# Two state-space heads in one kernel: k loaded in blocks of 32 partitions, a shift convolution by channel halves, and another instruction order

## The chip, the cores and the metric

The kernel runs on one core of a Trainium2 chip. Its time is the device time in microseconds of one execution; three executions of the kernel before gave a median of 419.54 us (419.09 to 419.80). The core's engines are TensorE (PE; PEld is its weight load), VectorE (DVE), ScalarE (ACT), GpSimd (POOL) and SyncE (SP), which here only issues DMAs.

## The reference

Two independent heads over 2048 time steps, 640 channels each; their outputs are concatenated.

```python
def A(x, ...):                       # S5 head: 640 complex states
    Lam_bar = exp(dt * Lam); B_bar = ((Lam_bar - 1) / Lam)[:, None] * Bmat
    Bu = einsum("bld,pd->blp", x, B_bar)
    h[t] = Lam_bar * h[t-1] + Bu[t]                 # scan over 2048 steps
    return 2 * einsum("blp,dp->bld", h, Cmat).real + x * Dskip
def B(q, k, v, shift_k, ssm_k, ssm_D):   # H3 head
    k_shift[t] = sum over 4 taps of k[t - j] * shift_k[:, j]
    kv = k_shift * v
    y = irfft(rfft(kv, 4096) * rfft(ssm_k, 4096))[:2048] + kv * ssm_D
    return q * y
```

## The kernel before, in words

**Everything lies in one SBUF tile, `arena`,** cut by hand into named columns (`LAY`). A recording layer (`Program.add`) takes each operation with the engines that may do it, and a table (`ORDER`) of entries such as `33G0` gives the order in which all operations are emitted: operation 33, on engine G (POOL), in PSUM bank 0. Each engine and the one DMA queue (SP's) run their entries strictly in this order. The profile names all of SBUF `arena` and all of PSUM `acc`; operations are told apart by their lines.

**Head A.** x is loaded as 16 blocks (`load_x`), transposed on PE, and B is scaled and transposed (`prep_B`, L497). The scan is a tree over 16 steps: on the way up, `up2`, `up1`, `up0` project x (L508, 200 matmuls of 512 columns) and combine neighbours (L527); `coarse` (L587 to L611) scans the 128 block totals by DVE; on the way down `down` (L628, L630, evicted at L646 and L648) spreads them; then `project` makes 16 output blocks C0 to C15 (L662, L667, evicted at L671, stored at L674). Its matrix C is first reordered in DRAM (L463) and transposed by a DMA (L464).

**Head B** is a long convolution by a two-step Fourier transform, done in two halves of 320 channels (0 and 1). Per half: the filter h is loaded (`load_h`, L716) and gets the skip weight D added (L705 loads it); `s1` (L793, evicted at L798) and `s2` (L811, evicted at L824) transform it; k and v are loaded (`load_k`, L729 and L732; `load_v`, L741); `conv` does the four taps and the product with v in 16 DVE operations (L767, L772, L773; one of the 32 stands on POOL); `s1`, `s2` transform kv; `product` (L835 to L842) multiplies spectra; `r2` (L856, evicted at L861) and `r1` (L877, with q at L889) go back, and four stores (L901) write a block. Called s1h, s1k, s2h, s2k with the half behind: s1k0 is the first step of kv in half 0.

**A tile of k or v has 4 blocks of 32 partitions,** one per 80 channels; a partition holds 64 time steps (and for k the 3 steps ahead of them, its overlap). Partition 0 of a block has no steps ahead of it: `load_k` zeroes them, loads partitions 1 to 31 of each block with their overlap in one DMA of 31x67 runs of 160 bytes (L729), and the 64 steps of the four first partitions in one DMA with a partition step of 32 (L732). `load_v` (L741) is a DMA of 32x64 such runs per block. Both halves use the same tiles, as do their taps (`T`). kv overwrites v, so that the weights of s1k are read with a step of 80 elements (160 bytes).

**Waits.** Eight DMA semaphores (DMAHW0 to DMAHW7) are given to the DMAs in turn, so each DMA waits until the one eight places ahead of it has landed.

Of the kernel before, what the change touches and what calls it, by code (L numbers as in the profile page):

```python
# [137 lines left out]
def act(n):  # L138
    return 0.20 + 0.00083 * n


def dve(n, rate=1.04):
    return 0.18 + 0.00104 * n * rate / 1.04
# [47 lines left out]
def setup(c):  # L191
# [62 lines left out]
    for ch in range(4):  # L254
# [12 lines left out]
        P.add("w_s", {A: 1.07}, lambda e, qc=qc, wo=wo: e.activation(out=wo, in_=qc, func=FN.Sin, bias=npi, scale=SC13),  # L267
# [20 lines left out]
    for ch in range(4):  # L288
# [6 lines left out]
        P.add("g_q", {G: 3.4}, lambda e, qc=qc: e.tensor_tensor(out=qc, in0=qc, in1=bc(f41s, [128, 1024]), op=ALU.mult),  # L295
              outs=[full], ins=[full, f41s])
        P.add("g_s", {A: 1.07}, lambda e, qc=qc: e.activation(out=sn, in_=qc, func=FN.Sin, scale=SC), outs=[sn], ins=[full])
        for el in range(2):
            go = Gt[:, ri, 32 * bh:32 * bh + 32, el, :]
            P.add("g_k", {V: .55, G: 1.3}, lambda e, go=go, el=el: e.tensor_scalar(  # L300
# [4 lines left out]
def params(c):  # L305
# [122 lines left out]
class PartA:  # L428
# [223 lines left out]
    def project(self, i):  # L652
# [21 lines left out]
        P.add(f"st_A{i}", {PSP: .17}, lambda e: e.dma_start(out=dst, in_=ys), ins=[ys], nbytes=128 * 1280)  # L674


class PartB:
    def __init__(self, c):
# [30 lines left out]
    def load_h(self, hf):  # L709
        c, P = self.c, self.c.P  # L710
        H = self.h[hf].rearrange("p (g b) -> p g b", b=64)
        for e_ in range(4):
# [3 lines left out]
            P.add(f"ld_h{hf}", {PSP: 2.9}, lambda e, d=d, src=src: e.dma_start(out=d, in_=src), outs=[d], nbytes=80 * 4096)  # L716
# [3 lines left out]
    def load_k(self, hf):  # L720
# [4 lines left out]
        for e_ in range(4):  # L725
            c0 = 320 * hf + 80 * e_
            d = K[32 * e_ + 1:32 * e_ + 32]
            src = bass.AP(self.k2.tensor, 61 * 640 + c0, [[64 * 640, 31], [640, 67], [1, 80]])
            P.add(f"ld_k{hf}", {PSP: 2.4}, lambda e, d=d, src=src: e.dma_start(out=d, in_=src), outs=[d], nbytes=31 * 67 * 160)  # L729
        d = K[0:128:32, 3:67, :]  # L730
        src = bass.AP(self.k2.tensor, 320 * hf, [[80, 4], [640, 64], [1, 80]])
        P.add(f"ld_k{hf}", {PSP: .35}, lambda e: e.dma_start(out=d, in_=src), outs=[d], nbytes=256 * 160)  # L732

    def load_v(self, hf):
        c, P = self.c, self.c.P
        Vt = self.vt[hf].rearrange("p (b g) -> p b g", g=80)
        for e_ in range(4):
# [3 lines left out]
            P.add(f"ld_v{hf}", {PSP: 2.4}, lambda e, d=d, src=src: e.dma_start(out=d, in_=src), outs=[d], nbytes=32 * 64 * 160)  # L741
# [11 lines left out]
    def conv(self, hf):  # L753
        c, P = self.c, self.c.P
        K = self.kt[hf].rearrange("p (b g) -> p b g", g=80)
        Vt = self.vt[hf].rearrange("p (b g) -> p b g", g=80)
        T1 = self.T[:, 2560:5120].rearrange("p (b g) -> p b g", g=80)
        T2 = self.T[:, 5120:7680].rearrange("p (b g) -> p b g", g=80)
        cost = {PDVE: dve(2560, .52), PPOOL: 5.6}
        for hb in range(2):  # L760
            b0 = 32 * hb
            t1, vv = T1, Vt[:, b0:b0 + 32]

            def tap(out, j):
# [8 lines left out]
            P.add(f"cv{hf}v", cost, lambda e, t1=t1, vv=vv: e.tensor_tensor(out=vv, in0=t1, in1=vv, op=ALU.mult), outs=[vv], ins=[t1, vv])  # L773

    def s1(self, what, hf, u):
# [19 lines left out]
        P.add(f"s1{what}{hf}_{u}", {PPE: .25}, mm, ins=lh + [c.F1], group=g, nmm=32)  # L795
# [5 lines left out]
    def s2(self, what, hf, ks):  # L801
# [12 lines left out]
        P.add(f"s2{what}{hf}_{ks[0]}", {PPE: 4 * n * .0345 + .02}, mm, ins=ins, group=g, nmm=4 * n)  # L814
# [29 lines left out]
    def r2(self, hf, u):  # L844
# [14 lines left out]
        P.add(f"r2{hf}_{u}", {PPE: .47}, mm, ins=ins, group=g, nmm=16)  # L859
# [4 lines left out]
    def r1(self, hf, bs):  # L864
# [20 lines left out]
        P.add(f"r1{hf}_{bs[0]}", {PPE: 8 * n * .0086 + .03}, mm, ins=ins, group=g, nmm=8 * n)  # L885
# [226 lines left out]
```

## Time and profile before

| | |
|---|---|
| median of 3 runs | 419.54 us (419.09 to 419.80) |
| the profiled execution's own time | 421.19 us |
| its span, first to last instruction | 419.4 us |
| PE busy / PEld | 233.0 / 162.7 us (56% / 39%) |
| DVE, ACT, POOL busy | 176.0, 148.1, 47.6 us (42%, 35%, 11%) |
| mean granted TensorE clock | 0.75 of full speed |
| DMA | 24.06 MB, 57 GB/s over the span |

The profiled execution took 1.8 us more than its span and 1.65 us more than the median, so a span is near the median of runs. An engine's idle time is put down to what released it; "SPq" is the queue's own issuing of DMAs, which counts as waiting, not as busy time. In two long stretches no engine computes.

### The profile page before, as it was taken

To read this page: it belongs to the slowest core of one execution; us is meant where nothing else is said; L and a number is where in the kernel's file an instruction comes from. 1 tells how busy PE (TensorE), PEld (TensorE's weight loads), DVE (VectorE), ACT (ScalarE), POOL (GpSimd) and SP (SyncE) were. 2 spreads that over 40 slices of the span, in tenths; PEclk is the share of its full clock that TensorE was granted. 3 is DMA by queue.
4 is the path that set the end of the run, shared out by engine and by line. 5 is a ranking of instruction groups with operands and counts; after the bars stand their busy time and mean duration, and the time that the engine had idled before them with its cause. 6 is when DMAs were issued, how large, how long until landed. Compare 5 with 4: busy or idle time off the path is not lost.

```text
span 419.4 us, 7914 instructions
## 1 busy us (share of the span) xinstructions
PE 233.0 (56%) x3576; PEld 162.7 (39%) x3576; DVE 176.0 (42%) x213; ACT 148.1 (35%) x175; POOL 47.6 (11%) x47
## 2 busy tenths in 40 slices
PE   3389899800000052998000000796696689999685
PEld 3355455500000021587000000554565578777563
DVE  5956810000000899254000000589794642299532
ACT  3659467400000310443000000685477543364421
POOL 5701300000000430000000000804104000000000
PEclk9969999965555565696555555799598886899989
DMA  6970000000005900061070002209270321032315
GB/s 200 228 107 7 18 17 17 17 15 15 21 15 84 131 0 9 15 85 21 15 163 15 15 15 41 41 0 169 37 125 15 59 64 50 2 107 68 95 34 143
DMA packets 96661, 24.06 MB, mean 57 GB/s; under 512 B 90996, under 2 KB 96628, under 8 KB 96628
## 3 DMA queue, kind: packets, MB, share of 16 engines
q1 hardware_dynamic: 96598, 23.56, 30.2%
q8 instruction: 28, 0.46, 0.5%
q14 instruction: 5, 0.04, 0.0%
q10 hardware_dynamic: 30, 0.00, 0.0%
HBM read 16.68 MB, written 6.88 MB: 56 GB/s over the span
## 4 chain that ended last, share of the span: by engine, by line
SPq 36%; PE 35%; DVE 12%; ACT 8%; issue 5%; DMA 2%; POOL 0%; ACTq 0%; POOLq 0%; DVEq 0%
SPq L729 16%; PE acc L662 11%; PE acc L793 7%; SPq L741 5%; SPq L700 5%; SPq L716 5%; SPq L464 4%; PE acc L811 4%; PE acc L508 3%; PE acc L856 3%; DVE arena L767 3%; DVE arena L772 2%; DMA arena<-in_B_k_dram 2%; ACT arena L824 2%; PE acc L628 2%
## 5 line engine op out<-in xcount | busy, mean ns | idle before, releaser
L824 ACT CAST arena<-acc 128x960 bf16<-128x960 f32 (+1 forms) x39 | 35.1, 916 | 89.0 <-DMA arena<-in_B_k_dram 68.5
L767 DVE TENSOR_TENSOR arena<-arena 128x2560 bf16<-128x2560 bf16 x16 | 26.0, 1643 | 79.9 <-POOL arena L706 79.6
L508 PE MATMUL acc<-arena 128*128 128x512 bf16 x200 | 53.9, 425 | 1.6 <-DVE arena L483 1.6
L628 PE MATMUL acc<-arena 128*128 128x512 bf16 (+2 forms) x47 | 16.3, 368 | 67.8 <-ACT arena L824 67.8
L662 PE MATMUL acc<-arena 128*128 128x320 bf16 x320 | 52.5, 316 | 0.0
L798 ACT CAST arena<-acc 128x1024 bf16<-128x1024 f32 x32 | 31.7, 1019 | 37.9 <-PE acc L793 37.9
L527 PE MATMUL acc<-arena 128*128 128x128 bf16 (+2 forms) x100 | 11.9, 254 | 53.2 <-DMA arena<-in_B_k_dram 53.2
L824 DVE CAST arena<-acc 128x960 bf16<-128x960 f32 (+1 forms) x7 | 7.1, 1012 | 71.8 <-DMA arena<-in_B_k_dram 66.5
L793 PE MATMUL acc<-arena 64*64 64x64 bf16 x1280 | 35.6, 264 | 2.4 <-DVE arena L243 1.7
L662 PEld LDWEIGHTS <-arena 128*128 128x128 bf16 x320 | 30.7, 103 | 13.4 <-issue 0.2
L793 PEld LDWEIGHTS <-arena 64*64 64x64 bf16 x1280 | 33.1, 189 | 6.9 <-issue 3.9
L811 PE MATMUL acc<-arena 128*64 128x160 bf16 x512 | 26.8, 262 | 13.8 <-DVE arena L600 13.0
L630 PEld LDWEIGHTS <-arena 128*128 128x128 bf16 x50 | 5.4, 110 | 71.4 <-issue 68.9
L295 POOL TENSOR_TENSOR arena<-arena 128x1024 int32<-128x1024 int32 x4 | 7.6, 1892 | 204.1 <-DMA arena<-in_B_k_dram 204.1
L508 PEld LDWEIGHTS <-arena 128*128 128x128 bf16 x200 | 20.1, 106 | 26.9 <-issue 10.4
L527 PEld LDWEIGHTS <-arena 128*128 128x128 bf16 x100 | 7.5, 100 | 57.9 <-issue 55.2
L811 PEld LDWEIGHTS <-arena 128*64 128x64 bf16 x512 | 22.2, 126 | 19.5 <-issue 18.4
L571 ACT CAST arena<-acc 128x256 bf16<-128x256 f32 (+1 forms) x9 | 3.7, 424 | 57.6 <-DMA arena<-in_B_k_dram 55.9
L856 PE MATMUL acc<-arena 64*128 64x128 bf16 x320 | 15.8, 264 | 11.3 <-ACT arena L861 4.8
L671 ACT CAST arena<-acc 128x640 bf16<-128x640 f32 x14 | 9.7, 692 | 32.1 <-PE acc L667 32.1
L861 ACT CAST arena<-acc 128x1024 bf16<-128x1024 f32 x14 | 14.1, 1015 | 16.4 <-PE acc L856 16.4
L889 DVE TENSOR_TENSOR arena<-acc,arena 128x960 bf16<-128x960 f32 (+1 forms) x12 | 12.2, 1043 | 16.8 <-PE acc L877 16.8
(134 smaller groups left out, 336.0 us busy)
## 6 DMA issues: line engine op xcount, KB each, us to landing
out_dram<-arena SPq DMA_DIRECT2D x32, 160.0 KB
arena<-in_B_k_dram SPq DMA_DIRECT2D x8, 324.5 KB
arena<-in_A_x_dram SPq DMA_DIRECT2D x16, 160.0 KB
arena<-in_B_ssm_k_dram SPq DMA_DIRECT2D x8, 320.0 KB
arena<-in_B_v_dram SPq DMA_DIRECT2D x8, 320.0 KB
arena<-in_B_q_dram SPq DMA_DIRECT2D x8, 320.0 KB
arena<-in_A_B_re_dram SPq DMA_DIRECT2D x2, 400.0 KB
arena<-in_A_B_im_dram SPq DMA_DIRECT2D x2, 400.0 KB
```

The source lines that it names most:

```text
L508: e.matmul(o, lhsT=self.BT[:, j, d, :], rhs=self.XT[:, d, t0:t0 + n], start=(d == 0), stop=(d == 4), skip_group_check=True)
L628: e.matmul(B[:, o:o + 128 * k], lhsT=c.I3[:, 0:128], rhs=A[:, j, m + q:m + q + k, 0:128], start=True, stop=False, skip_group_check=True)
L662: e.matmul(B[:, 512 * b:512 * b + 320], lhsT=lh[j], rhs=self.CT[:, j, 320 * b:320 * b + 320], start=(j == 0), stop=False, skip_group_check ...
L700: P.add("ld_sk", {PSP: .2}, lambda e, d=d, src=src: e.dma_start(out=d, in_=src), outs=[d], nbytes=128 * 640)
L716: P.add(f"ld_h{hf}", {PSP: 2.9}, lambda e, d=d, src=src: e.dma_start(out=d, in_=src), outs=[d], nbytes=80 * 4096)
L729: P.add(f"ld_k{hf}", {PSP: 2.4}, lambda e, d=d, src=src: e.dma_start(out=d, in_=src), outs=[d], nbytes=31 * 67 * 160)
L767: P.add(f"cv{hf}m", cost, lambda e: e.tensor_tensor(out=out, in0=k, in1=bc(s, [128, 32, 80]), op=ALU.mult), outs=[out], ins=[k, c.SK[:, hf ...
L793: e.matmul(B[64 * b:64 * b + 64, 512 * l + 64 * i:512 * l + 64 * i + 64], lhsT=lh[i][ps], rhs=F[ps, b, :], start=True, stop=True, tile_pos ...
L798: P.add(f"e1{what}{hf}_{u}", {PACT: act(1024), PDVE: dve(1024)}, lambda e, B: c.CP[e](out=out, in_=B.rearrange("p (l n k s) -> p k s l n", ...
L811: e.matmul(B[64 * s:64 * s + 64, 512 * b + 160 * i:512 * b + 160 * i + 160], lhsT=c.W[:, k, 64 * b:64 * b + 64], rhs=self.AS[:, k, 160 * s ...
L824: c.CP[e](out=out, in_=b.rearrange("p r (k j n) -> p r k j n", k=n, j=4) if nj > 1 else b.rearrange("p r (k x) -> p r k x", k=n))
L856: e.matmul(B[:, 512 * s + 128 * i:512 * s + 128 * i + 128], lhsT=lh[i][s][r], rhs=rh, start=(r == 0), stop=(r == 1), tile_position=(64 * s ...
```

## The change

Three edits. In `load_k`, four DMAs of 32 partitions and 64 steps take the place of the four of 31 partitions and of the one for the first partitions; four small DMAs (`ld_kh`, L734) load the overlap of partitions 1 to 31. In `conv`, an operation takes all 64 steps of 40 channels where it took 32 steps of 80; kv goes to `T` (two areas) and not over v, and s1k reads its weights there with a step of 40 elements (80 bytes). Third, the planning costs are other numbers (in many lines, which do nothing at run time) and so is the `ORDER` table.

```diff
 def act(n):
-    return 0.20 + 0.00083 * n
+    return 0.16 + 0.000833 * n
...
+        self.kv = [v("T", 2560, 2560), v("T", 0, 2560)]
...
         for e_ in range(4):
             c0 = 320 * hf + 80 * e_
-            d = K[32 * e_ + 1:32 * e_ + 32]
-            src = bass.AP(self.k2.tensor, 61 * 640 + c0, [[64 * 640, 31], [640, 67], [1, 80]])
-            P.add(f"ld_k{hf}", {PSP: 2.4}, ...)
-        d = K[0:128:32, 3:67, :]
-        src = bass.AP(self.k2.tensor, 320 * hf, [[80, 4], [640, 64], [1, 80]])
-        P.add(f"ld_k{hf}", {PSP: .35}, ...)
+            d = K[32 * e_:32 * e_ + 32, 3:67, :]
+            src = self.k2.rearrange("(a b) d -> a b d", b=64)[:, :, c0:c0 + 80]
+            P.add(f"ld_k{hf}", {PSP: 1.6}, ...)
+        for e_ in range(4):
+            d = K[32 * e_ + 1:32 * e_ + 32, 0:3, :]
+            src = bass.AP(self.k2.tensor, 61 * 640 + 320 * hf + 80 * e_, [[64 * 640, 31], [640, 3], [1, 80]])
+            P.add(f"ld_kh{hf}", {PSP: .5}, ...)
...
-        for hb in range(2):
-            b0 = 32 * hb
-            t1, vv = T1, Vt[:, b0:b0 + 32]
+        for h in range(2):
+            t1 = self.kv[h].rearrange("p (b n) -> p b n", n=40)
+            hs = slice(40 * h, 40 * h + 40)
+            vv = Vt[:, :, hs]
...
-                k = K[:, 3 - j + b0:3 - j + b0 + 32, :]
+                k = K[:, 3 - j:67 - j, hs]
...
-            P.add(f"cv{hf}v", cost, ... tensor_tensor(out=vv, in0=t1, in1=vv, op=ALU.mult), outs=[vv], ins=[t1, vv])
+            P.add(f"cv{hf}v", cost, ... tensor_tensor(out=t1, in0=t1, in1=vv, op=ALU.mult), outs=[t1], ins=[t1, vv])
...
-            K = self.vt[hf].rearrange("p (b g) -> p b g", g=80)
-            lh = [K[:, :, x] for x in gs]
+            lh = [self.kv[x // 40].rearrange("p (b n) -> p b n", n=40)[:, :, x % 40] for x in gs]
...
 ORDER = (
-    "33G0 76V0 100G0 0G0 160S0 79S0 25V0 115V0 101G0 80S0 6G0 9V0 10V0 7V0 26V0 54V0 55V0 8V0 12V0 77A0 1G0 2V0 78S0 81T0 24V0 3V0 "
+    "48G0 0G0 111V0 115V0 151S0 25V0 76V0 99G0 14V0 154S0 112V0 1G0 27V0 100G0 6G0 113V0 114V0 77A0 38G0 24V0 80A0 43G0 7V0 54V0 8V0 "
...
```

What the table moves is seen in three places. Line numbers from L705 on are one to three higher in the kernel after.

**SP, the first half's k and v.** In the queue's order before, behind the filter loads (the semaphores that an issue waits for stand in brackets):

```order
L729 DMA arena<-in_B_k_dram 31x67x80 [waits DMAHW6_49,Activation_49]
L729 DMA arena<-in_B_k_dram 31x67x80 [waits DMAHW7_49]
L729 DMA arena<-in_B_k_dram 31x67x80 [waits DMAHW0_49]
L700 DMA arena<-in_B_shift_k_dram 128x1x320 [waits DMAHW1_49]
L729 DMA arena<-in_B_k_dram 31x67x80 [waits DMAHW2_49]
L741 DMA arena<-in_B_v_dram 32x64x80 [waits DMAHW3_49]
L732 DMA arena<-in_B_k_dram 4x64x80 [waits DVE_49,DMAHW4_49,Activation_49,Pool_49]
L741 DMA arena<-in_B_v_dram 32x64x80 [waits DMAHW5_49]
```

and after, again behind the filter loads (two more k loads, one `ld_kh` and two v loads follow, and one of the two DMAs of C stands among them):

```order
L730 DMA arena<-in_B_k_dram 32x64x80 [waits DMAHW5_49,Activation_49]
L743 DMA arena<-in_B_v_dram 32x64x80 [waits DMAHW6_49]
L453 DMA arena<-in_A_x_dram 128x640 [waits DMAHW7_49]
L743 DMA arena<-in_B_v_dram 32x64x80 [waits DMAHW0_49]
L734 DMA arena<-in_B_k_dram 31x3x80 [waits DMAHW1_49,Pool_49]
L734 DMA arena<-in_B_k_dram 31x3x80 [waits DMAHW2_49]
L730 DMA arena<-in_B_k_dram 32x64x80 [waits DMAHW3_49]
L730 DMA arena<-in_B_k_dram 32x64x80 [waits DMAHW4_49]
L734 DMA arena<-in_B_k_dram 31x3x80 [waits DMAHW5_49]
L701 DMA arena<-in_B_shift_k_dram 128x1x320 [waits DMAHW6_49]
```

The DMA with a partition step of 32 (4x64x80), which waited for three engines, is gone from k; the load of D (4x80, not shown) has the same step and remains.

**ACT, an eviction of the up pass** (L571, `ev_up0c_4`, which writes no part of k). Before, it waits for semaphore DMAHW4, whose holder is the 4x64x80 load above:

```order
L571 CAST arena<-acc 128x2x128 [waits PE_49]
L523 CAST arena<-acc 128x8x128 [waits PE_49]
L571 CAST arena<-acc 128x256 [waits DMAHW4_49,PE_49]
L824 CAST arena<-acc 128x2x3x4x40 [waits PE_49,Activation_49] x2
L546 CAST arena<-acc 128x2x4x128 [waits PE_49]
```

and after:

```order
L571 CAST arena<-acc 128x2x128 [waits PE_49]
L826 CAST arena<-acc 128x2x3x4x40 [waits Activation_49]
L279 ACTIVATE arena<-arena 128x192 [waits DVE_49]
L571 CAST arena<-acc 128x256 [waits PE_49]
L826 CAST arena<-acc 128x2x3x4x40 [waits PE_49,Activation_49] x3
```

No operation of the up pass waits for a k load any more.

**DVE, the end of the first convolution.** Before, the convolution's last operations are followed by the coarse scan (L600, L587):

```order
L767 TENSOR_TENSOR arena<-arena 128x2560
L772 TENSOR_TENSOR arena<-arena 128x2560
L773 TENSOR_TENSOR arena<-arena 128x2560
L600 TENSOR_TENSOR arena<-acc,arena 128x640
L587 COPY arena<-arena 128x1280
```

and after, evictions of the up pass (L571) stand between:

```order
L775 TENSOR_TENSOR arena<-arena 128x2560
L571 CAST arena<-acc 128x2x2x128
L776 TENSOR_TENSOR arena<-arena 128x2560 x2
L571 CAST arena<-acc 128x2x128
L571 CAST arena<-acc 128x256
L603 TENSOR_TENSOR arena<-arena 128x640
L826 CAST arena<-acc 128x2x3x4x40
```

The first of these evictions (`ev_up0a_2`) is the operation that PE's next combination waits for. In half 1, one tap and one product with v of the convolution stand on POOL after the change; before, one addition.

## Rows read from the trace of the kernel before

**Rows 1.** Stages: start:end, length, busy PE PEld DVE ACT POOL, PEclk, DMA share, GB/s
```profile
0.00:25.80 25.80, 10.68 (x95) 9.93 (x96) 19.52 (x55) 14.25 (x21) 13.40 (x31) 0.87 0.95 204
25.80:82.30 56.50, 54.44 (x690) 29.29 (x690) 21.11 (x30) 35.46 (x42) 4.92 (x4) 0.97 0.11 20
82.30:135.50 53.20, 0.03 (x1) 0.00 (x0) 0.00 (x0) 0.00 (x0) 0.00 (x0) 0.55 0.17 28
135.50:164.70 29.20, 7.54 (x28) 2.69 (x28) 26.04 (x18) 6.13 (x7) 8.61 (x5) 0.56 0.46 53
164.70:197.40 32.70, 31.82 (x457) 23.63 (x456) 15.09 (x26) 13.38 (x15) 0.00 (x0) 0.72 0.28 40
197.40:264.20 66.80, 0.07 (x4) 0.10 (x1) 0.42 (x1) 0.00 (x0) 0.00 (x0) 0.52 0.23 45
264.20:268.90 4.70, 3.63 (x44) 3.25 (x44) 1.97 (x2) 3.93 (x5) 4.66 (x2) 0.58 0.23 38
268.90:339.70 70.80, 55.20 (x1089) 38.92 (x1086) 53.56 (x47) 47.00 (x53) 16.02 (x6) 0.83 0.41 66
339.70:368.90 29.20, 29.06 (x451) 23.67 (x450) 8.68 (x8) 9.48 (x11) 0.00 (x0) 0.82 0.11 33
368.90:388.40 19.50, 19.50 (x228) 14.84 (x226) 18.61 (x20) 9.83 (x13) 0.00 (x0) 1.00 0.30 86
388.40:419.40 31.00, 21.01 (x504) 16.40 (x501) 10.99 (x12) 8.67 (x10) 0.00 (x0) 0.93 0.38 92
```

**Rows 2.** Timeline of SP's queue: start, time to issue, line, count:
```profile
2.29 5.10 SPq L453 DMA_DIRECT2D arena<-in_A_x_dram  x11
...
13.09 12.18 SPq L716 DMA_DIRECT2D arena<-in_B_ssm_k_dram  x4
...
39.97 45.05 SPq L729 DMA_DIRECT2D arena<-in_B_k_dram  x3
...
107.57 22.91 SPq L741 DMA_DIRECT2D arena<-in_B_v_dram  x1
130.65 1.21 SPq L732 DMA_DIRECT2D arena<-in_B_k_dram  x1
131.91 4.91 SPq L741 DMA_DIRECT2D arena<-in_B_v_dram  x3
...
190.16 25.73 SPq L464 DMA_TRANSPOSE arena<-c_planes  x1
```

**Rows 3.** Stretches chosen for DMA; the last column is GB/s:
```profile
90.00:106.00 16.00, 0.00 (x0) 0.00 (x0) 0.00 (x0) 0.00 (x0) 0.00 (x0) 0.50 0.08 15
...
131.90:139.00 7.10, 1.01 (x2) 0.10 (x1) 0.72 (x1) 3.11 (x4) 3.33 (x3) 0.50 1.27 160
```

**Rows 4.** Longest waits: who for whom, us in total, times, longest:
```profile
ACT arena L571 <- DMA arena<-in_B_k_dram: 55.9, 1, 55.9
...
PE acc L527 <- DMA arena<-in_B_k_dram: 53.2, 1, 53.2
```

**Rows 5.** DVE by line: busy us, mean ns | idle before:
```profile
L767 DVE TENSOR_TENSOR arena<-arena 128x2560 bf16<-128x2560 bf16 x16 | 26.0, 1643 | 79.9 <-POOL arena L706 79.6
...
L835 DVE TENSOR_TENSOR arena<-arena 128x2560 bf16<-128x2560 bf16 x8 | 11.9, 1493 | 0.8
```

**Rows 6.** PE and PEld in L508 (matmuls of 512 columns) by stage, PEclk, DMA:
```profile
25.80:82.30 56.50, 41.00 (x170) 16.04 (x169) 0.97 0.11 20
...
164.70:197.40 32.70, 8.46 (x20) 2.58 (x20) 0.72 0.28 40
```

**Rows 7.** The same for L793 (s1):
```profile
25.80:82.30 56.50, 3.82 (x320) 3.15 (x320) 0.97 0.11 20
164.70:197.40 32.70, 14.02 (x320) 13.30 (x320) 0.72 0.28 40
...
339.70:368.90 29.20, 13.43 (x320) 13.05 (x320) 0.82 0.11 33
```

**Rows 8.** The same for L856 (r2, weights of 128 columns):
```profile
388.40:419.40 31.00, 6.76 (x160) 5.97 (x160) 0.93 0.38 92
```

More of the change, by code (lines that the diff above doesn't have):

```diff
@@ L266, in setup @@
         wo = Wt[:, 8 * ch:8 * ch + 8, :].rearrange("p k c -> p (k c)")
-        P.add("w_s", {A: 1.07}, lambda e, qc=qc, wo=wo: e.activation(out=wo, in_=qc, func=FN.Sin, bias=npi, scale=SC13),
+        P.add("w_s", {A: 1.15}, lambda e, qc=qc, wo=wo: e.activation(out=wo, in_=qc, func=FN.Sin, bias=npi, scale=SC13),
               outs=[wo], ins=[qc, npi])
@@ L294, in setup @@
             channel_multiplier=0), outs=[full])
-        P.add("g_q", {G: 3.4}, lambda e, qc=qc: e.tensor_tensor(out=qc, in0=qc, in1=bc(f41s, [128, 1024]), op=ALU.mult),
+        P.add("g_q", {G: 1.9}, lambda e, qc=qc: e.tensor_tensor(out=qc, in0=qc, in1=bc(f41s, [128, 1024]), op=ALU.mult),
               outs=[full], ins=[full, f41s])
@@ L446, in load_B @@
             s = src.rearrange("(j m) d -> m j d", m=64)[:, j0:j0 + 5, :]
-            P.add(f"ld_B{half}", {PSP: .4}, lambda e, dst=dst, s=s: e.dma_start(out=dst, in_=s), outs=[dst], nbytes=64 * 5 * 1280)
+            P.add(f"ld_B{half}", {PSP: .62}, lambda e, dst=dst, s=s: e.dma_start(out=dst, in_=s), outs=[dst], nbytes=64 * 5 * 1280)
     def load_x(self, i):
@@ L452, in load_x @@
         s = self.x2.rearrange("(s r) d -> r s d", r=16)[ROW0[i]]
-        P.add(f"ld_x{i}", {PSP: .17}, lambda e: e.dma_start(out=dst, in_=s), outs=[dst], nbytes=128 * 1280)
+        P.add(f"ld_x{i}", {PSP: .45}, lambda e: e.dma_start(out=dst, in_=s), outs=[dst], nbytes=128 * 1280)
     def load_C(self):
@@ L673, in project @@
         dst = c.out.rearrange("(s r) d -> r s d", r=16)[ROW0[i]][:, 0:640]
-        P.add(f"st_A{i}", {PSP: .17}, lambda e: e.dma_start(out=dst, in_=ys), ins=[ys], nbytes=128 * 1280)
+        P.add(f"st_A{i}", {PSP: .5}, lambda e: e.dma_start(out=dst, in_=ys), ins=[ys], nbytes=128 * 1280)
 class PartB:
@@ L715, in load_h @@
             src = c.ins["B_ssm_k"][c0:c0 + 80, :].rearrange("g (a b) -> a g b", b=64)
-            P.add(f"ld_h{hf}", {PSP: 2.9}, lambda e, d=d, src=src: e.dma_start(out=d, in_=src), outs=[d], nbytes=80 * 4096)
+            P.add(f"ld_h{hf}", {PSP: 3.0}, lambda e, d=d, src=src: e.dma_start(out=d, in_=src), outs=[d], nbytes=80 * 4096)
         x = H[:, :, 0]
@@ L740, in load_v @@
             src = self.v2.rearrange("(a b) d -> a b d", b=64)[:, :, c0:c0 + 80]
[L741 removed]
+            P.add(f"ld_v{hf}", {PSP: 1.6}, lambda e, d=d, src=src: e.dma_start(out=d, in_=src), outs=[d], nbytes=32 * 64 * 160)
     def load_q(self, hf):
@@ L772, in conv @@
                 P.add(f"cv{hf}a", cost, lambda e, t1=t1: e.tensor_tensor(out=t1, in0=t1, in1=T2, op=ALU.add), outs=[t1], ins=[t1, T2])
-            P.add(f"cv{hf}v", cost, lambda e, t1=t1, vv=vv: e.tensor_tensor(out=vv, in0=t1, in1=vv, op=ALU.mult), outs=[vv], ins=[t1, vv])
+            P.add(f"cv{hf}v", cost, lambda e, t1=t1, vv=vv: e.tensor_tensor(out=t1, in0=t1, in1=vv, op=ALU.mult), outs=[t1], ins=[t1, vv])
     def s1(self, what, hf, u):
@@ L794, in mm @@
                                  stop=True, tile_position=(64 * l, 64 * b))
-        P.add(f"s1{what}{hf}_{u}", {PPE: .25}, mm, ins=lh + [c.F1], group=g, nmm=32)
+        P.add(f"s1{what}{hf}_{u}", {PPE: .26 if what == "h" else .46}, mm, ins=lh + [c.F1], group=g, nmm=32)
         gh, n0 = u // 5, 8 * (u % 5)
@@ L813, in s2 @@
         ins = [c.W[:, k, :] for k in ks] + [self.AS[:, k, :] for k in ks]
-        P.add(f"s2{what}{hf}_{ks[0]}", {PPE: 4 * n * .0345 + .02}, mm, ins=ins, group=g, nmm=4 * n)
+        P.add(f"s2{what}{hf}_{ks[0]}", {PPE: 4 * n * .0345}, mm, ins=ins, group=g, nmm=4 * n)
         if what == "h":
```

37 lines of the change are left out of this document (18 added, 19 removed), and 67 rows, old and new, of the table ORDER.

## The prediction

> **What bounds the kernel now.** I read the busy time by stage first. The stage borders are where a view changes: PE's first `up2` (25.8 us), two points at which every engine stops (82.3 and 197.4) and resumes (135.5 and 264.2), the end of the first convolution (164.7), and in the second part the start of the first product (268.9), of s1k1 (339.7), of the second product (368.9) and its end (388.4) [rows 1]. In two of these stages, 53.2 and 66.8 us long, all engines together are busy for less than 1 us: 120.0 of 419.4 us hold no work.
>
> The queue's timeline says why. Issuing three of the k loads takes 45.05 us, and a v load that stands behind them takes 22.91, where three v loads of about the same size take 4.91 when nothing is ahead of them [rows 2]. While k loads run, the core moves 15 GB/s; with v loads in their place, 160 [rows 3]. A k load is 31x67 runs of 160 bytes, 332 KB: at 15 GB/s that is 22 us, and there are eight. That the engines stop, though much of their next work needs no k, is seen in the waits: the eviction L571 on ACT and PE's L527 both end a wait of over 53 us on a k load [rows 4]; the eviction's semaphore belongs to L732, the load of the first partitions. It was issued at 130.65, behind the slow loads [rows 2], and the stall ended 4.9 us later. The second stall repeats this with half 1.
>
> Between the stalls the bound changes. In 25.8 to 82.3 PE is busy 54.4 of 56.5 us. In 135.5 to 164.7 it is DVE with the convolution (26.0 of 29.2) while PE does 28 matmuls. In 164.7 to 197.4 it is PE again (31.8 of 32.7) at a granted clock of 0.72. In 268.9 to 339.7 PE and DVE are both near three quarters (55.2 and 53.6 of 70.8); after that PE [rows 1].
>
> **The change, part by part.**
>
> *k loads.* The new shape, 32x64 runs of 160 bytes, is v's: 1.64 us to issue (4.91 / 3) and 2.0 us of transfer at 160 GB/s [rows 2, 3]. The `ld_kh` loads are 31x3 runs each. Bounds: 15 KB take 0.1 us at 160 GB/s, 1.0 us at 15 GB/s; eight of them 1 to 8 us in all, spread over a queue that is not full. I take 1.0 each, nearest to the old row, since 31 partitions stay. The Trainium skill (page "DMA: Bandwidth & Descriptors", section "Why a DMA increments its semaphore by 16 and not by 1") has a DMA use the largest number of engines up to 16 that divides its slowest dimension: 16 for 32, one for 31. By that rule the overlap loads still go through one engine each, as I assumed, and the sum is the same.
>
> When does the first half's k land? SP issues the load of D, then the filter loads (4 at 3.05 = 12.2 us), five x loads (0.46 each, 2.3), and k and v up to the last k load (four k and two v at 1.64, the rest about 3: 12.8) [rows 2]. D's issue waits for the start-up's parameter chain, so not past 25.8; the last k load is out by 53 and landed by 56 us. `conv` is 14 DVE operations up to the eviction that PE waits for (`ev_up0a_2`), then two more. Its runs are now 40 channels long; the product's L835 has runs of 40 too and takes 1493 ns, the taps mean 1643 [rows 5]: 14 take 21 to 23 us, so it ends by 79, and PE comes to that eviction's user at about 82. DVE has room: 21.1 us used of 56.5, and 26 more is 47. If k lands later, PE stalls by as much; that cover is some 3 us thick.
>
> *First stall:* 53.2 goes to 0. *The convolution's stage* (29.2) goes: DVE's part moves under the up pass, and 28 matmuls remain, 10 of them of 512 columns at 0.24 us (41.0 / 170) [rows 6], the others 1.5 together: 4 us.
>
> *164.7 to 197.4.* s1k0 took 14.0 us of PE here, s1h0 with the same 320 matmuls and contiguous weights 3.8 [rows 7]. So the weights' step costs: 13.3 us for 320 loads of 64 columns at 160 bytes, 0.65 ns a column, against 5.97 for 160 loads of 128 columns in r2, whose step is 80 bytes: 0.29 ns [rows 7, 8]. With an 80-byte step s1k0 should take 320 x 64 x 0.29 = 6.0, with ends 6.5 us; bounds 3.8 and 14.0. Gain 7.5. The Trainium skill (page "SBUF — State Buffer", section "Door 1: The DMA port swizzle (why `[64,N]` ≈ `[32,N]`)") says that a stride is free only while reads stay in a 16-byte line. Both steps leave the line each time, so by this rule s1k gains nothing and each half keeps its 14 us; r2's rows say otherwise, and that case is a rival below. Second, the 20 large matmuls took 8.46 us here (0.423 each) where 0.241 is paid at the higher clock [rows 6]; this stage now follows a busy PE and not a stall, so I take 3.6 back. PE needs 32.7 - 7.5 - 3.6 = 21.6; with evictions of 1.0 us behind matmuls of 0.65, ACT (13.4) and DVE (15.1) wait for each other more: I take 24, bounds 21.6 and 28.
>
> *Second stall:* 66.8 goes to 0, since k of half 1 loads while the coarse scan runs. 264.2 to 268.9 stays 4.7. So the first product starts at 25.8 + 56.5 + 4 + 24 + 4.7 = 115 us, where it was 268.9.
>
> *268.9 to 339.7 (70.8).* The same work in another order, and C5 in it. The bounds are PE's 55.2, the busiest engine, and 75 (no better, and q or h late). POOL now takes two of the convolution's operations (5 us each there, beside DVE). The gaps of before are PE waiting for evictions and DVE; the new table mixes r2, s1h and `down` more finely. I take 66, near the old order.
>
> *339.7 to 368.9 (29.2, PE busy 29.1).* s1k1 13.4 becomes 6.5 and C5 has moved ahead: 22.3 less some 3 is 19.5; but s1k needs 10 evictions of 1.0 to 1.2 us on two engines; I take 20, bounds 15 and 29. *368.9 to 388.4* is the product on DVE (18.6 of 19.5) with six C blocks on PE: 19.5. *The tail* (31.0) has r2, r1, three C blocks and the last stores as before: 29, bounds 25 and 33.
>
> **Sum:** 115 + 66 + 20 + 19.5 + 29 = 249.5 of span. The profiled execution's time lies 1.8 us above its span and 1.65 above the median, which cancel: **249 us**. With all lower bounds 225, with all upper ones 277.
>
> **The rivals.**
>
> *Tighter:* the new order packs PE to its busiest-engine bound. 25.8 + 54.4 + 4 + 21.6 + 4.7 + 55.2 + 16 + 19.5 + 26 = 227 us. For it: PE was 96% busy in the up pass. Against it: DVE and ACT are at 75% in 268.9 to 339.7, and every hand-over costs.
>
> *Strided weights stay slow:* what limits s1k is any step beyond a line, and r2 is fast for another reason (128 columns a load). Then 7.5 in each half comes back: 264 us. For it, the page above; against it, [rows 8].
>
> *The transposing load of C holds the queue.* Its issue took 25.73 us [rows 2], with a k load still moving ahead of it. If that is its own cost, it starts when `up0a_8` has freed its target, about 98 us, C is there at about 126, and PE stands at C0 (next to the first product) for some 9 us, with h of half 1 and D behind it in the queue: 259, and 270 with late loads.
>
> *Not faster.* If the 32-partition loads still ran through one DMA engine, the eight of them would cost 22 us each as before, and the eight overlap loads 1 us each on top: 420 to 428, slower. It decides when nearly all eight are slow, since each one accounts for 22 of the 170 us. Against it: the same shape as v's, which ran at 160 GB/s.
>
> **How the numbers follow.** Chances: my case (235 to 262) 0.58; tighter 0.14; strided weights slow 0.13; C or other loads late 0.13; not faster 0.02. The range from 231 to 270 leaves out half of "tighter", a part of the late loads, the last case and a little of my own: 0.18. A difference of 0.2% (0.8 us) is what a measurement here can tell from none. Faster: all but the last case, 0.98; same and slower 0.01 each.
>
> **What would show it right or wrong.** No stretch longer than 5 us without work; SP's k issues at 1.6 us; conv0 beside PE's L508; the first product at about 115 us; L793 in s1k at 6 to 7 us per 320 matmuls; a granted clock near 0.9. Wrong if the first product starts after 125 (loads late or the clock low), if C0 waits for the transposing load, or if the second half of the kernel, 134 us here, keeps its 150.

## The result and the profile after

The kernel after takes 253.25 us (median of four runs, 250.75 to 257.22), 0.601 of the kernel before (95% interval 0.596 to 0.606). The highest of the four runs was in a slower state of the chip, and the ratio leaves it out. The prediction was 249 us, its range 231 to 270. The profiled execution took 252.43 us, with a span of 250.6 us.

Busy time by stage of the kernel after; columns as in [rows 1]. The last borders are the same events: the first product starts at 111.4, s1k1 at 174.2, the second product at 196.5, and it ends at 216.4. At 26.6 TensorE's last wait of the start ends; the first `up2` runs ahead of it here, from 16.9 us, with 30 of the 200 large matmuls. The border at 84.1 is where the point of 82.3 of before is passed without a stop; 20 large matmuls of the up pass are left there, where 30 were:

```profile
0.00:26.60 26.60, 15.63 (x131) 10.87 (x131) 21.11 (x61) 17.60 (x24) 14.22 (x32) 1.00 0.82 178
26.60:84.10 57.50, 51.23 (x670) 28.13 (x670) 47.42 (x42) 35.84 (x44) 14.97 (x9) 0.94 0.76 107
84.10:111.40 27.30, 27.16 (x508) 20.42 (x509) 17.35 (x27) 17.71 (x21) 2.85 (x1) 0.94 0.73 110
111.40:174.20 62.80, 51.30 (x1117) 37.80 (x1112) 49.55 (x48) 44.09 (x51) 14.71 (x4) 0.95 0.48 81
174.20:196.50 22.30, 21.18 (x448) 19.36 (x449) 13.14 (x10) 14.03 (x16) 0.00 (x0) 0.86 0.30 77
196.50:216.40 19.90, 19.90 (x208) 15.11 (x205) 18.81 (x20) 8.04 (x10) 0.00 (x0) 0.99 0.07 26
216.40:250.60 34.20, 24.01 (x502) 19.12 (x499) 12.03 (x11) 8.24 (x10) 0.00 (x0) 0.75 0.34 83
```

The two stages without work, 120.0 us in [rows 1], are gone, and so is the stage of the first convolution: in 26.6 to 84.1 VectorE is busy for 47.4 us where it was for 21.1, beside nearly the same work of TensorE (670 matmuls, before 690). The last row is the one that grew, from 31.0 to 34.2 us, at a granted clock of 0.75 instead of 0.93.

The queue's timeline after answers [rows 2] (start, time to issue, line, count):

```profile
28.42 0.66 SPq L730 DMA_DIRECT2D arena<-in_B_k_dram  x1
...
36.75 2.77 SPq L730 DMA_DIRECT2D arena<-in_B_k_dram  x2
...
98.63 6.47 SPq L464 DMA_TRANSPOSE arena<-c_planes  x1
```

A k load leaves the queue in 0.7 and in 1.4 us here, and the transposing load of C in 6.47 where it took 25.73. VectorE's first tap starts at 53.29, so k was there; v is first needed by a product at 79.57. One overlap load runs alone: issued at 70.17, its 15 KB move between 71.2 and 72.3 (columns as in [rows 1]):

```profile
71.20:72.30 1.10, 1.10 (x23) 0.74 (x20) 1.07 (x2) 1.07 (x3) 1.10 (x1) 1.00 0.07 13
```

That is nearly the 15 GB/s of the old k loads [rows 3], for 31 partitions with 3 steps each and not 67. So the number of steps is not what makes the old shape slow, and the 1.0 us of the prediction for such a load held.

S1 by stage (the columns of [rows 7]), with s1k0 in the first row and s1k1 in the second:

```profile
84.10:111.40 27.30, 10.89 (x320) 10.12 (x320) 0.94 0.73 110
...
174.20:196.50 22.30, 10.15 (x320) 9.79 (x319) 0.86 0.30 77
```

s1k takes 10.9 and 10.2 us, between the 14 of before and the 6.5 of the forecast.

### The profile page after: what moved, and what is told of

It reads as the page before. It is cut to its first block, busy times and chain, and to the rows that moved or that the text cites. A ratio compares the mean times of both kernels' runs of the same rounds, so it can differ in the third digit from the quotient of the medians.

```text
span 250.6 us, 7891 instructions
## 1 busy us (share of the span) xinstructions
PE 210.4 (84%) x3566; PEld 150.8 (60%) x3566; DVE 179.4 (72%) x217; ACT 145.5 (58%) x173; POOL 46.8 (19%) x45
## 5 line engine op out<-in xcount | busy, mean ns | idle before, releaser
L508 PE MATMUL acc<-arena 128*128 128x512 bf16 x200 | 50.0, 402 | 5.5 <-ACT arena L483 2.6
L662 PE MATMUL acc<-arena 128*128 128x320 bf16 x320 | 49.5, 304 | 0.1
L826 ACT CAST arena<-acc 128x960 bf16<-128x960 f32 (+1 forms) x39 | 34.7, 919 | 9.7 <-PE acc L813 5.5
L662 PEld LDWEIGHTS <-arena 128*128 128x128 bf16 x320 | 29.8, 99 | 11.3
L508 PEld LDWEIGHTS <-arena 128*128 128x128 bf16 x200 | 19.3, 102 | 28.6 <-issue 7.1
L795 PE MATMUL acc<-arena 64*64 64x64 bf16 x1280 | 29.6, 244 | 5.8 <-DVE arena L719 2.8
L795 PEld LDWEIGHTS <-arena 64*64 64x64 bf16 x1280 | 27.4, 165 | 10.4 <-issue 4.2
L770 DVE TENSOR_TENSOR arena<-arena 128x2560 bf16<-128x2560 bf16 x15 | 23.7, 1594 | 0.3
L858 PEld LDWEIGHTS <-arena 64*128 64x128 bf16 x320 | 13.9, 153 | 13.0 <-DVE arena L863 7.2
L775 DVE TENSOR_TENSOR arena<-arena 128x2560 bf16<-128x2560 bf16 x12 | 18.8, 1567 | 0.3
L863 DVE CAST arena<-acc 128x1024 bf16<-128x1024 f32 x7 | 8.6, 1225 | 9.3 <-PE acc L858 7.7
L840 DVE TENSOR_TENSOR arena<-arena 128x1280 bf16<-128x1280 bf16 x16 | 12.9, 823 | 2.7 <-DMA arena<-in_B_ssm_D_dram 1.9
L646 ACT CAST arena<-acc 128x1024 bf16<-128x1024 f32 (+2 forms) x16 | 13.9, 931 | 0.8 <-PE acc L630 0.8
L837 DVE TENSOR_TENSOR arena<-arena 128x2560 bf16<-128x2560 bf16 x8 | 11.9, 1492 | 1.6 <-ACT arena L826 0.9
```

What stands on the lines that cost most here:

```text
L508: e.matmul(o, lhsT=self.BT[:, j, d, :], rhs=self.XT[:, d, t0:t0 + n], start=(d == 0), stop=(d == 4), skip_group_check=True)
L646: e.copy(out=o, in_=b)
L662: e.matmul(B[:, 512 * b:512 * b + 320], lhsT=lh[j], rhs=self.CT[:, j, 320 * b:320 * b + 320], start=(j == 0), stop=False, skip_group_check ...
L775: P.add(f"cv{hf}a", cost, lambda e, t1=t1: e.tensor_tensor(out=t1, in0=t1, in1=T2, op=ALU.add), outs=[t1], ins=[t1, T2])
L795: e.matmul(B[64 * b:64 * b + 64, 512 * l + 64 * i:512 * l + 64 * i + 64], lhsT=lh[i][ps], rhs=F[ps, b, :], start=True, stop=True, tile_pos ...
L826: c.CP[e](out=out, in_=b.rearrange("p r (k j n) -> p r k j n", k=n, j=4) if nj > 1 else b.rearrange("p r (k x) -> p r k x", k=n))
```

## The experiments

Four questions: are the slow transfers or the DMA with a partition step the cause of the stalls (e1 to e4); what a strided weight costs (e6, e7, e9, e10); why the tail grew (e8, e11); do the answers add up (e12). e5 is the kernel after once more. Ratios are to the kernel before on the same chip.

**e1: the loads alone, in the old order.** The k loads of the kernel after in the kernel before; the four overlap loads stand where L732 stood.

```diff
-            d = K[32 * e_ + 1:32 * e_ + 32]
+            d = K[32 * e_:32 * e_ + 32, 3:67, :]
...
-        d = K[0:128:32, 3:67, :]
+        ds = [K[32 * i + 1:32 * i + 32, 0:3, :] for i in range(4)]
```

> The kernel before, in its own order and with its own convolution, with the k loads alone changed to four of 32 partitions and four overlap loads. Theory (the two stalls are the loads, the order only takes what they leave): both stalls go (53.2 and 66.8 us) and the first convolution starts on VectorE about 60 us, where VectorE is free, and ends about 85, beside the up pass, so that of the stage of 29.2 us some 4 remain: 419.5 - 120 - 25 = 275 us, between 268 and 290. Rival (the searched order hides the loads): the stalls become shorter but stay, and the time lies above 320.

Measured: 267.87 us, ratio 0.640 (0.635 to 0.645). VectorE's timeline in e1, the first and the last lines of the first convolution:

```profile
58.90 2.88 DVE L771 TENSOR_TENSOR arena<-arena 128x2560 bf16<-128x2560 bf16 x2
...
81.41 1.49 DVE L777 TENSOR_TENSOR arena<-arena 128x2560 bf16<-128x2560 bf16 x1
```

The convolution ends at 82.9 us, when the up pass has not ended: the old order already gives it that place once k is there. The loads alone are worth 150 us (418.06 on this chip to 267.87); order and convolution add 15 (267.87 to 253.25 by the medians, 16 by the ratios 0.640 and 0.601). By stage e1 and the kernel after differ by 7.1 us up to the first product (118.6 and 111.4), 5.9 up to s1k1, 6.3 up to the second product, and in the tail e1 is 3.6 us shorter.

**e2: fast loads, and the load with the partition step kept.** As e1, with one more load behind the overlap loads. It is called the barrier below, since it waits for three engines and they wait for it:

```diff
+        ds.append(K[0:128:32, 3:67, :])
+        ss.append(bass.AP(self.k2.tensor, 320 * hf, [[80, 4], [640, 64], [1, 80]]))
```

> As e1, but the load of the four first partitions with its partition step of 32 (4x64x80) stays behind the fast loads (it writes once more what they wrote). Theory: the load with the step costs what its waits cost, and not its transfer; fast loads are there by 50 us, so it is held by ScalarE's and GpSimd's earlier work alone, until 60 to 78 us. TensorE loses 0 to 5 us, but the convolution, which stands behind GpSimd's work that waits for it, starts about 80 and ends about 105, and 10 to 20 of the 25 us come back: 285 to 295 us. Rival (the step itself is what stops the engines): most of the 120 us stays, over 380.

Measured: 305.47 us, ratio 0.731 (0.725 to 0.737), above the expected 295. In the queue's timeline of e2 the five loads (four overlaps, then the load with the step):

```profile
48.30 30.76 SPq L737 DMA_DIRECT2D arena<-in_B_k_dram  x5
```

the queue's longest wait ahead of these loads (columns as in [rows 4]):

```profile
SPq L737 <- ACT arena L523: 21.0, 1, 21.0
```

and GpSimd's and VectorE's timelines, the waits in brackets:

```profile
81.64 1.89 POOL L295 TENSOR_TENSOR arena<-arena 128x1024 int32<-128x1024 int32 x1 [37.77 <-DMA arena<-in_B_k_dram]
...
84.25 4.57 DVE L773 TENSOR_TENSOR arena<-arena 128x2560 bf16<-128x2560 bf16 x2 [26.89 <-POOL arena L706]
```

The load was held until 79 us, in the end by ScalarE (VectorE stood from 57 and GpSimd from 44), GpSimd stood until 81.6 for it, and the convolution started at 84 instead of 59 us. That is the chain that was expected, with a larger price: TensorE then stood for 9.9 and 13.8 us for VectorE's work among and behind the convolution, where 0 to 5 us had been expected. The barrier costs 37.6 us beside e1, and 34.7 of them are there when the first product starts (153.2 and 118.6). The barrier alone does not make the stalls of before: with fast loads 113 us are gone (418.06 to 305.47).

**e3: slow loads, without the partition step.** The kernel before, the first partitions in four DMAs of one partition:

```diff
-        d = K[0:128:32, 3:67, :]
+        ds = [K[32 * i:32 * i + 1, 3:67, :] for i in range(4)]
```

> The kernel before with its slow loads of 31 partitions, but the four first partitions come in four DMAs of one partition each, so that no DMA with a partition step of 32 stands among the k loads. Theory (the transfers are the cost): the convolution still gets k at about 130 us, and VectorE's coarse scan stands behind it, so the first stall loses 4 us at most; at the second the first product can go ahead, until the filter of half 1, queued behind the slow loads, is missed: some 30 us come back. 419.5 - 34 = 385 us, 360 to 405. Rival (the barrier is the cost, slow loads could be hidden): below 330.

Measured: 400.76 us, ratio 0.958 (0.951 to 0.965). The long waits of TensorE in its timeline:

```profile
139.85 0.61 PE L597 MATMUL acc<-arena 128*128 128x512 bf16 x1 [58.92 <-DVE arena L207]
...
271.29 1.50 PE L860 MATMUL acc<-arena 64*128 64x128 bf16 x24 [38.57 <-DVE arena L844]
```

Without the barrier the first wait comes back in another place: TensorE's part of the coarse scan now stands for 58.9 us for a copy (L207) that VectorE has among the convolution's operations, and those wait for k (76.9 us). The second wait is for the first product on VectorE, which itself waits:

```profile
263.83 0.82 DVE L842 TENSOR_TENSOR arena<-arena 128x1280 bf16<-128x1280 bf16 x1 [40.92 <-DMA arena<-in_B_ssm_D_dram]
```

The product reads nothing of D. But D's load, issued at 260.1 us behind the k loads, has the same partition step of 32, so e3 still has a load of the barrier's kind, and what taking out both kinds would give was not run. Taking the barrier of k alone away is worth 17 us, the slow loads alone 113, both 150: each hides a part of the other.

**e4: the kernel after with slow loads.** Four loads of 31x67 runs and four of one partition, in the new order:

```diff
-            d = K[32 * e_:32 * e_ + 32, 3:67, :]
+            ds = [K[32 * e_ + 1:32 * e_ + 32], K[32 * e_:32 * e_ + 1, 3:67, :]]
```

> The kernel after, with the loads of 31x67 runs back and the first partitions by DMAs of one partition (no overlap loads). Theory: k of half 0 lands at about 28 + 4 x 22 = 116 us where it landed at about 53; the convolution ends about 140 and the eviction behind it holds TensorE for some 60 us; k of half 1 then lands at about 205, about when its convolution is due. 253 + 60 = 313 us, up to 335 with the queue's later loads held. Rival (the order hides slow loads): under 275.

Measured: 389.29 us, ratio 0.929 (0.920 to 0.937): far above the 313 expected. TensorE's long waits:

```profile
149.38 0.80 PE L527 MATMUL acc<-arena 128*128 128x128 bf16 x6 [64.22 <-DVE arena L571]
...
227.47 2.85 PE L662 MATMUL acc<-arena 128*128 128x320 bf16 x10 [44.68 <-DMA arena<-c_planes]
...
269.97 1.17 PE L798 MATMUL acc<-arena 64*64 64x64 bf16 x64 [19.60 <-POOL arena L719]
```

and the queue:

```profile
146.35 44.02 SPq L734 DMA_DIRECT2D arena<-in_B_k_dram  x4
190.48 3.88 SPq L746 DMA_DIRECT2D arena<-in_B_v_dram  x3
194.40 24.60 SPq L734 DMA_DIRECT2D arena<-in_B_k_dram  x2
219.11 6.16 SPq L464 DMA_TRANSPOSE arena<-c_planes  x1
```

The first wait is the one expected. What I had not counted is what stands behind k of half 1 in the queue: the load of C, out at 219 us, and the filter of half 1. C's own issue takes 6.16 us here too. So the new order does not hide slow loads; with them, order and convolution together are worth 11.5 us (400.8 to 389.3).

**e5: the kernel after again.**

> The kernel after, unchanged, beside the next three on the same chip: 253 us, 250 to 257 as in its four runs.

Measured: 252.52 us (251.15 to 255.12, six runs), ratio 0.600 (0.597 to 0.603). e6 to e8 are told against it.

**e6: weights of s1k with a step of 160 bytes.**

```diff
-            t1 = self.kv[h].rearrange("p (b n) -> p b n", n=40)
+            t1 = self.T[:, 0:5120].rearrange("p (b n) -> p b n", n=80)[:, :, hs]
```

> The kernel after, with the two areas of kv interleaved in T, so that s1k reads its weights with a step of 160 bytes again; convolution, loads and order as after. Theory (the step sets the time of a weight load at any clock): a load of 64 columns takes 42 ns where it took 31, 320 of them in each half 3.5 us more, on TensorE, which is the bound in both stages: 253 + 7 = 260 us. Rival (the 14 us of before came from the low granted clock, 0.72 and 0.82 there, and any step beyond a line costs the same): the same 31 ns and 253 us.

Measured: 261.89 us, ratio 0.623 (0.620 to 0.626), 9.4 us more. TensorE's timeline, s1k1:

```profile
183.50 5.34 PE L795 MATMUL acc<-arena 64*64 64x64 bf16 x128
193.97 6.62 PE L795 MATMUL acc<-arena 64*64 64x64 bf16 x160
```

6.62 / 160 is 41.4 ns a load; the kernel after has 10.15 / 320 = 31.7. The 320 loads of each half took 14.16 and 13.43 us, where the kernel after has 10.89 and 10.15: 6.6 of the 9.4 us. The rest shows in the C blocks beside s1k1 (L662, columns as in [rows 7]), first in the kernel after, then in e6:

```profile
174.20:196.50 22.30, 6.06 (x40) 3.61 (x40) 0.86 0.30 77
```

```profile
177.30:206.70 29.40, 9.67 (x40) 4.93 (x40) 0.71 0.23 59
```

The same 40 matmuls took 3.6 us more, at a lower granted clock; why the clock was lower there is not shown. The step sets the price of a load, and going from 160 to 80 bytes was worth it: of the 15 us that order and convolution add to e1, some 9 are this step.

**e7: contiguous weights.**

```diff
-            P.add(f"cv{hf}v", ... tensor_tensor(out=t1, in0=t1, in1=vv, op=ALU.mult), ...)
+            pk = self.kp[h].rearrange("p (n b) -> p b n", n=40)
+            P.add(f"cv{hf}v", ... tensor_tensor(out=pk, in0=t1, in1=vv, op=ALU.mult), ...)
```

> The kernel after, with the convolution's last operation (the product with v) writing kv with steps innermost, so that s1k reads contiguous weights; scratch areas change places and the product of the first channel half comes before the taps of the second. Theory: s1k takes 4.3 us in each half as s1h does, where it took 10.9 and 10.2; VectorE pays for the strided write, 1.5 us become up to 2.7 in three operations, beside TensorE; with evictions behind it a gain of 8 to 10 us, 244 us. Rival (the strided write costs more than the read, or the evictions set the pace): 251 to 258 us.

Measured: 276.15 us, ratio 0.655 (0.651 to 0.659), 23.6 us slower, more than the rival gave. By form:

```profile
L778 DVE TENSOR_TENSOR arena<-arena 128x2560 bf16<-128x2560 bf16 x3 | 35.7, 11915 | 0.1
```

The product takes 11.9 us where it took 1.49. It writes single elements 128 bytes apart. In s1k the 32 loads of a group took 0.45 us, so that half of the theory held, but TensorE waits for VectorE, the longest times 10.3 us (at 100.4) and 10.6 us (at 211.3).

**e9: a price list.** s1k reads its weights with ten different steps, and three products write runs of 8, 20 and 4 channels into the scratch area; the spectra of head B are not the reference's here.

```diff
-            lh = [self.kv[x // 40]...[:, :, x % 40] for x in gs]
+            st = (1, 2, 4, 8, 16, 20, 24, 32, 36, 40)[u]
```

> The kernel after as a measuring device: each of the ten groups of s1k reads its 32 weights of 64 columns with a step of its own (1, 2, 4, 8, 16, 20, 24, 32, 36 and 40 elements of 2 bytes), and three of the products with v write runs of 8, 20 and 4 channels with a step of 64 such runs between them into the scratch area; the values of head B's spectra are not the reference's. Theory A (time grows with the step): a load of 64 columns takes 11 to 14 ns at a step of 1 and rises evenly to 31 at 40 elements, some 17 at 16. Theory B (a line of 16 bytes): flat at 11 to 14 ns up to 8 elements, and flat again near 31 beyond it. For VectorE, where the write with a step of 128 bytes and runs of one element took 11.9 us: runs of 20 elements 1.5 us, of 8 between 1.5 and 2.7, of 4 between 2.7 and 6.

Measured: 249.16 us in one run, of which only durations are read. S1 in stretches of TensorE (columns as in [rows 7], the weight loads second): two groups at 2 and 4 bytes; five at 64, 72, 40, 80 and 48 bytes; one at 8 bytes; one at 16:

```profile
176.68:177.19 0.51, 0.51 (x61) 0.51 (x64) 1.00 0.00 0
...
182.21:187.20 4.99, 4.98 (x160) 4.84 (x160) 0.94 0.49 123
95.56:96.30 0.74, 0.68 (x32) 0.57 (x32) 1.00 0.00 0
100.48:101.63 1.15, 1.15 (x32) 1.03 (x32) 1.00 2.76 264
```

and VectorE, the products with runs of 8 and of 20:

```profile
79.07 3.01 DVE L779 TENSOR_TENSOR arena<-arena 128x2560 bf16<-128x2560 bf16 x2
```

Per load: 8 ns (0.51 / 64) up to 4 bytes, 18 (0.57 / 32) at 8 bytes, 32 (1.03 / 32) at 16 bytes, and 30 (4.84 / 160) in the mean from 40 to 80. That is neither theory as it stood: the rise is a step, as in B, but it lies between 4 and 16 bytes and not beyond 16; with e6 there is a second rise, to 41 ns at 160. VectorE pays nothing for runs of 20, 8 or 4 channels (1.49 us for the run of 4 as well), where up to 6 us had been expected.

**e10: kv in runs of four channels.** As e7, with a step of 8 bytes:

```diff
+            pk = self.kp[h].rearrange("p (g b n) -> p b g n", b=64, n=4)
```

> As e7 (the product with v writes another layout, scratch areas change places), but kv is written in runs of 4 channels, so that the weights of s1k have a step of 8 bytes. Theory, by e9: the product keeps its 1.5 us, a weight load takes 13 to 18 ns where it took 31, s1k 4.3 to 5.7 us where it took 10.9 and 10.2; both stages have TensorE as their bound, so 253 - 8 = 245 us, less if the ten evictions behind s1k set the pace. Rival (evictions set the pace at once): 250 to 253 us.

Measured: 243.26 us (240.67 to 245.59), ratio 0.578 (0.574 to 0.581); the products with v, then S1 in the stages of s1k0 and s1k1 (columns as in [rows 7]):

```profile
L779 DVE TENSOR_TENSOR arena<-arena 128x2560 bf16<-128x2560 bf16 x3 | 4.5, 1493 | 0.1
```

```profile
83.50:104.20 20.70, 6.17 (x320) 5.39 (x320) 1.00 0.90 136
168.60:187.80 19.20, 5.58 (x320) 5.13 (x319) 0.84 0.35 89
```

It is about 9 us faster than the kernel after (ratios 0.578 and 0.600), and s1k accounts for them: 6.2 and 5.6 us where it took 10.9 and 10.2. The loads cost 16 to 17 ns, as the theory had it; evictions did not take the gain back.

**e8: C blocks between the operations of r2 in the tail.** Only entries of `ORDER` and their PSUM banks change.

```diff
-... 655T2 656V2 667T6 668A6 651T0 652V0 539S0 661T4 662A4 649T2 ...
+... 655T2 656V2 667T6 668A6 651T0 652V0 539S0 661T4 662A4 734T2 735A2 649T6 ...
```

> The kernel after, with two of the last three C blocks put between the operations of the second half's r2 (other PSUM banks for some of them), the third before r1. Theory (the tail lost 5 us because TensorE waits for evictions in r2 and its granted clock then falls to 0.61): the granted clock stays above 0.9, r2's matmuls take 7 us instead of 8.8, the C blocks fill the waits, and the tail of 34 us becomes 27 to 30: 247 to 249 us. Rival (the tail is set by 20 evictions on two engines, the clock costs nothing): 252 to 254 us.

Measured: 255.53 us, ratio 0.609 (0.605 to 0.612): no gain, by the medians 3.0 us more than e5. TensorE's timeline in the tail of e8:

```profile
217.50 0.74 PE L858 MATMUL acc<-arena 64*128 64x128 bf16 x16 [0.89 <-DVE arena L863]
219.63 1.07 PE L858 MATMUL acc<-arena 64*128 64x128 bf16 x16 [1.39 <-DVE arena L863]
220.64 2.41 PE L662 MATMUL acc<-arena 128*128 128x320 bf16 x10
```

The waits of r2 stand as they stood (0.88 and 1.39 us in the kernel after), the granted clock of the tail (215.4 to 252.3) is 0.83 and not above 0.9, and the C block between runs at half the clock at first (2.41 us for ten matmuls, 1.52 elsewhere). Filling is no cure when the waits are of another making: r2 rotates over four pairs of banks, and yet it waits for an eviction of one or two groups ago.

**e11: r2 evicted to another area.** In the program of the kernel after, weight loads of r2 wait for evictions of other groups: the third group of the tail, in banks 0 and 1, waits for that of the first, out of banks 2 and 3. An eviction of group u writes columns 4u to 4u+3 of each 40 in Y, and the third group reads others. Here the second half's evictions go to AS:

```diff
-        self.Z = v("Y").rearrange("p (x s n) -> p x s n", s=2, n=40)
+        self.Z = [v(x).rearrange("p (x s n) -> p x s n", s=2, n=40) for x in ("Y", "AS")]
```

> The kernel after, but the evictions of the second half's r2 go to the area AS, free by then, and not over the columns of Y that r2 has read; the same order and banks. In the program of after, some r2 weight loads wait for the eviction of the group before, though it wrote other columns of Y; here they wait for PSUM banks alone. Theory (these waits make r2 of the tail slow, 14 us for 8.8 us of matmuls, and open the gaps behind which the granted clock falls): r2 takes 10 to 11 us, the tail 30 to 31: 249 us. Rival (the evictions themselves set the pace): 252 to 254 us.

Measured: 241.96 us (241.13 to 244.69), ratio 0.578 (0.574 to 0.581). That is 10.6 us less than e5 by the medians and 9 by the ratios, which allow for the other chip. The stages of r2 and of what follows it, first in the kernel after, then in e11 (columns as in [rows 1]):

```profile
217.00:232.20 15.20, 8.85 (x166) 7.69 (x165) 6.12 (x5) 6.16 (x7) 0.00 (x0) 0.63 0.26 66
232.20:250.60 18.40, 14.56 (x334) 11.03 (x333) 5.91 (x6) 2.08 (x3) 0.00 (x0) 0.84 0.42 101
```

```profile
216.10:222.80 6.70, 5.60 (x166) 5.37 (x165) 5.75 (x5) 6.20 (x7) 0.00 (x0) 1.00 0.60 149
222.80:239.30 16.50, 12.01 (x334) 9.23 (x334) 5.91 (x6) 2.08 (x3) 0.00 (x0) 1.00 0.46 112
```

TensorE's timeline of r2, first one of its five waits in the kernel after, then the whole r2 in e11, and then the part of r2 in the kernel after from 222.0 us on (columns as in [rows 1]):

```profile
221.25 2.35 PE L858 MATMUL acc<-arena 64*128 64x128 bf16 x40 [1.39 <-DVE arena L863]
```

```profile
216.13 5.56 PE L858 MATMUL acc<-arena 64*128 64x128 bf16 x160
```

```profile
222.00:232.20 10.20, 6.13 (x107) 5.26 (x103) 3.67 (x3) 3.96 (x4) 0.00 (x0) 0.50 0.08 21
```

r2 takes 6.7 us instead of 15.2, its 160 matmuls run in one piece, VectorE evicts its five groups without a gap (5.75 us), and the granted clock is 1.00 where it was 0.63 and 0.84. The gain is larger than expected, since the clock came back in the stage behind r2 as well. So the fall of the clock followed from the waits, and both together were the tail.

**e12: e10 and e11 together.**

> The kernel after with the changes of e10 and e11 together. They act on different stages (s1k of both halves; the tail's r2), so by the theory that each takes away a cost on the path the gains add: 253 - 10 - 11 = 232 us, 229 to 236. Rival (one gain uses up the other, by the clock or the queue of stores): 238 to 243 us.

Measured: 232.98 us (231.61 to 235.23), ratio 0.554 (0.551 to 0.558): the gains add, and this is the fastest version.

## Why the prediction was right, and where it was not

**The mechanism was right.** Both stalls were the k loads, and they went as forecast (e1, e3). That the convolution moves under the up pass was right too, and without TensorE waiting: its 14 operations ran from 53.3 to 76.9, and the eviction behind them waited 2.1 us for TensorE and not for k. e1 shows that the new order was not needed for it. The change as a whole is some 150 us of loads and 15 of order and convolution.

**The barrier was weighed too lightly.** The prediction put all eight times 22 us on the transfers and named the barrier (L732) only as the reason that the stop is general. e2 prices it apart: 37.6 us with fast loads, since it must wait for ScalarE, and GpSimd and the convolution wait for it.

**Up to the first product** 115 was forecast, 111.4 measured. The term "4 + 24 + 4.7" was 32.7 and came to 27.3, although s1k0 in it took 10.9 and not 6.5. Ten of its large matmuls, 2.4 us, run ahead of the border here (84.1, where 82.3 was forecast); beyond that I had left room for evictions that was not needed, TensorE is busy there for 27.16 of 27.30 us.

**The step that failed first: the price of a strided weight.** I carried 0.29 ns a column from r2 to s1k, because both read with 80 bytes; s1k has 31 ns for 64 columns, 0.49. The Trainium skill (page "SBUF — State Buffer", section "Door 1: The DMA port swizzle (why `[64,N]` ≈ `[32,N]`)") calls a stride free only while reads stay in a 16-byte line. In e9 16 to 80 bytes cost the same (32 and 30 ns), as by that rule, but 8 bytes cost more than 4 (18 against 8 ns), and in e6 160 more than 80 (41 against 31 ns), which the rule does not give. So the rival that kept 14 us was wrong as well; the truth lay in the middle, 3.7 to 4.4 us above my term in each half. Why r2, with 128 columns a load, gets them at 35 ns (5.6 us for 160 in e11) stays open.

**The load of C** took 6.47 us to issue; C0 waited for nothing. The 25.73 of before belonged to the k loads ahead: in e1, where they alone are changed, it is 7.47. And e4 shows how much hangs behind them in the queue.

**The middle** (66 forecast) took 62.8, s1k1's stage (20) 22.3, the product (19.5) 19.9.

**The step that failed second: the tail,** 29 forecast with bounds of 25 and 33, 34.2 measured. I had taken the 31.0 of before for the same work less some waits. It is the same work, but its r2 waits for evictions in a chain: before four times, 3.6 us in all, and in the kernel after five times, 5.2 us, with a granted clock of 0.63 there. e11 shows that the waits were the cause: without them the whole tail is 23.2 us (216.1 to 239.3).

That the sum came out 1.1 us from the span is luck, since the errors cancel: -3.6 up to the first product, -3.2 in the middle, +2.3, +0.4 and +5.2. Two slips did not bear on it: the bounds as stated add up to 227 and 276, not 225 and 277, and in 268.9 to 339.7 ScalarE was busy for 66% of the time, not 75 [rows 1].

## What to carry to other kernels

Count what each load makes wait, not only how long it lasts: a slow shape, a barrier by its partition step and the work queued behind either one hide each other, and taking one away shows the next. Before filling an idle gap, ask whether the wait in it is real: evictions into columns that lie between those still to be read cost 10 us here, and another target area was enough. A layout is best priced on both sides at once, the writer's and the reader's: runs of four channels cost the writer nothing and the reader a good half of what forty did.

## What was not expected of the hardware

A VectorE product of 2560 elements takes 1.49 us with runs of 4, 8, 20 and 40 elements in its output, and 11.9 us with single elements 128 bytes apart; on GpSimd single elements made 6.3 us into 11.7 (5.0 with runs of four, in e10). A weight load of 64 columns takes 8 ns at a step of up to 4 bytes, 18 at 8, 30 to 32 from 16 to 80 and 41 to 43 at 160, the last at either clock (before the change 2.75 us for 64 at a granted clock of 1.00, and 5.36 us for 128 at 0.70). In the tail of the kernel after, TensorE waited for 0.88 and 1.39 us, and behind that, from 222.0 to 232.2, the granted clock was 0.50, the lower of its two levels (1.2 of 2.4 GHz); in e11, where the same matmuls ran in one piece, it stayed at 1.00.
